# The output transfers of an eight-batch attention and gating kernel, issued from GpSimd's queue in the place of SyncE's

## The chip, the core and the metric

The kernel runs on one core of one Trainium2 chip. The metric is the device time of one execution in microseconds (us); lower is better. The core has TensorE (PE, with its weight loads as PEld), VectorE (DVE), ScalarE (ACT), GpSimd (POOL) and SyncE (SP). Each of them works through its own instructions in order. Transfers are issued by an instruction on one of the engines, and 16 DMA engines move the bytes.

## The reference

Eight batches, eight heads, 576 positions, 64 columns a head. Linear attention with a norm, then a gated feed-forward layer that mixes positions:

```python
kv = np.einsum('bhsd,bhse->bhde', k, v)
out = np.einsum('bhsd,bhde->bhse', q, kv)
rms = np.sqrt(np.mean(out * out, axis=-1, keepdims=True) + 1e-06)
out = out / rms * g_norm
x = out.transpose(0, 2, 1, 3).reshape(8, 576, 512)
h = np.maximum(x @ w_in, 0.0)                 # 512 -> 1024
u, v = h[..., :512], h[..., 512:]
v_n = (v - mean(v)) / np.sqrt(var(v) + 1e-06)
v_s = np.einsum('ts,bsd->btd', w_spatial, v_n) + b_spatial[None, :, None]
return (u * v_s) @ w_out                      # (8, 576, 512) float32
```

## The kernel before

**Tiling.** 576 positions are four blocks of 128 and a tail of 64. The tails of two batches, an even one and the odd one after it, share one block of 128. Every large product is made of three products of high and low parts (`hl`), which ACT makes by a rounding cast and DVE by a subtraction (`split`, lines 499 and 500); two of them, the one for `u` and the mix over positions, use a scheme of seven block products instead of eight (`seven`, `sp_steps`).

**Passes.** After an opening that decodes and splits the weights, `run` works through one batch at a time. In the text, pass b is that of batch b: `x_sums` makes sums of the attention output and splits them into the tiles `T` and `UX` (four ACT casts, line 499), `hv` makes `v` (psums `psh`, ACT line 469, DVE 475), `hv_tail` does the same for the tail block of two batches, `u_steps` makes `u` (psums `psua`, `psub`, `psuc`), `sp_steps` mixes and gates into `G`, and `out_unit` multiplies by `w_out`. The attention of batch b+1 (`pskv`, `KVB`, psums `pso` of line 190, `xx`, `xt`, `pstr`, `pstt`, ending in `XH` and `XL`) is mixed into pass b.

**The output.** `out_unit(b, c)` runs 12 matmuls into a PSUM bank (`pso` of line 463, one of four in the pool `ps_mm`), copies the bank to a tile `o` on ACT (line 805) and stores it. `o` is one of two buffers of the tag `stg`, which the attention tile `xt` of an odd batch shares. A pass ends with blocks 0, 1, 2, 3 where b is even, and with 0, 1, the shared tail block, 2, 3 where b is odd. So from the third block on a copy waits until an earlier `o` has been stored. The tail block is stored by two transfers of 64 rows (lines 809 and 810). Only the very last block is copied half by ACT and half by DVE (lines 802 and 803).

**What shares buffers.** `UX` and the output weight `WO` are one buffer, as are `T` and `G`: the load of `UX` (three transfers, line 1038, issued by POOL) waits for the last output matmul of the pass before, the casts into `T` as well; the load of `WO` (two transfers, line 1044, POOL) waits for the last use of `UX`. POOL also moves the tail tiles `TB` (line 549) and, in pass 1, stores three weight sums to `spare_u` (line 625).

**The order.** Within each engine the order is set by a scheduler that walks the program with a cost model of its own and picks what it takes to be ready; tokens in strings such as `EVEN` and `ODD` give the order in which the steps are written. A change of an instruction's engine can so move others.

Of the kernel before, what the change touches and what calls it, by code (L numbers as in the profile page):

```python
# [16 lines left out]
B, H, S, D = 8, 8, 576, 64  # L17
DM, FF = 512, 1024
FH = FF // 2
P = 128  # L20
NP = H // 2
NC = S // P
TAIL = S - NC * P
# [54 lines left out]
def body(ctx: ExitStack, tc, qT, kvm, kvt, g2, w_in, wsT, bsp, w_out, out):  # L78
    nc = tc.nc
# [379 lines left out]
    def three(ps, pairs):  # L459

        n = len(pairs)
        for i, (lt, rh) in enumerate(pairs):
            nc.tensor.matmul(ps, lt, rh, start=i == 0, stop=i == n - 1)  # L463

    def hl(lh, ll, rh, rl):
        return [(lh, rh), (lh, rl), (ll, rh)]
# [324 lines left out]
    def out_unit(b, c):  # L791
        ps = ps_mm.tile([P, 512], F32, name="pso2", tag="mm")
        cols = slice(c * P, (c + 1) * P)
        three(ps, [m for k in range(4) for m in
                   hl(*((GH[:, k, cols], GL[:, k, cols]) if c < NC else (GT[:, 0, k], GT[:, 1, k])),
                      WO[:, 0, k], WO[:, 1, k])])
        if (b, c % 2) == (B - 1, 0):
            o = work.tile([P, DM], F32, name="o", tag="v", bufs=3)
        else:
            o = work.tile([P, DM], F32, name="o", tag="stg", bufs=2)  # L800
        if (b, c) == (B - 1, NC - 1):
            nc.scalar.copy(o[:, 0:HALF], ps[:, 0:HALF])
            nc.vector.tensor_copy(o[:, HALF:DM], ps[:, HALF:DM])
        else:
            nc.scalar.copy(o, ps)  # L805
        if c < NC:
            nc.sync.dma_start(out[b, c * P:(c + 1) * P, :], o)
        else:
            nc.sync.dma_start(out[b - 1, NC * P:S, :], o[0:TAIL])
            nc.sync.dma_start(out[b, NC * P:S, :], o[TAIL:P])  # L810

# [298 lines left out]
    def outs(b):  # L1112
        return [lambda c=c: out_unit(b, c) for c in [0, 1] + [NC] * (b % 2) + [2, 3]]
# [54 lines left out]
```

## Time and profile before

| | |
|---|---|
| median of 3 runs | 487.5 us (487.13 to 489.95) |
| the profiled execution, its own time | 489.41 us |
| its span in the trace | 487.6 us |
| PE busy | 474.9 us, 97% |
| DVE busy | 381.4 us, 78% |
| ACT busy | 274.8 us, 56% |
| POOL busy | 35.8 us, 7% |
| TensorE's granted clock over the span | 0.997 |
| DMA queue of SP | 47.25 MB, 29.2% of 16 engines' span |
| DMA queue of POOL | 25.87 MB, 16.3% |

The profiled execution took 489.41 us, of which 1.8 us lie outside the span of its trace. It is 1.9 us above the median. Busy times are those of the trace; the ends of matmuls are modelled, so matmuls that follow each other overlap in the rows.

### The profile page before, as it was taken

How to read it: one execution, taken by the hardware profiler on the slowest of the kernel's cores; microseconds unless marked ns; L12 is line 12 of the kernel's file. 1: busy time of each engine (PE TensorE's matmuls, PEld its weight loads, DVE VectorE, ACT ScalarE, POOL GpSimd, SP SyncE). 2: the span in 40 equal slices, each digit the busy share in tenths (PEclk: the TensorE clock that was granted, in tenths of full speed). 3: DMA queues.
4: the chain of work that ended last, by engine and by line, in shares of the span. 5: the costliest groups of instructions: out<-in, count | busy, mean ns of one | idle time of the engine just before them, and what ended most of it. 6: DMA issues, size and time to landing. Idle time of an engine off the chain costs nothing.

```text
span 487.6 us, 10839 instructions
## 1 busy us (share of the span) xinstructions
PE 474.9 (97%) x4140; PEld 427.1 (88%) x4140; DVE 381.4 (78%) x1035; ACT 274.8 (56%) x824; POOL 35.8 (7%) x71
## 2 busy tenths in 40 slices
PE   6999989999999999999999999999999999999996
PEld 6889979998988899889988889888998889988995
DVE  2899787984994899869893899968986689986870
ACT  4898734975526773366533686257742578346322
POOL 5001100000211010000001001010000101010000
PEclk9999989999999999999999999999999999999999
DMA  8999331653159224390626616264323703333403
GB/s 284 375 301 318 90 99 67 184 182 109 65 174 315 87 77 173 123 333 12 217 85 196 206 46 206 84 218 164 116 103 130 239 1 80 128 88 128 149 26 108
DMA packets 30199, 74.16 MB, mean 152 GB/s; under 512 B 6626, under 2 KB 9698, under 8 KB 28612
## 3 DMA queue, kind: packets, MB, share of 16 engines
q1 hardware_dynamic: 24468, 47.25, 29.2%
q0 software_dynamic: 5456, 25.87, 16.3%
q8 instruction: 32, 0.52, 0.4%
q10 hardware_dynamic: 224, 0.36, 0.2%
q14 instruction: 19, 0.16, 0.1%
HBM read 58.09 MB, written 13.11 MB: 146 GB/s over the span
## 4 chain that ended last, share of the span: by engine, by line
PE 75%; DVE 11%; ACT 7%; DMA 4%; issue 2%; SPq 0%; ACTq 0%; DVEq 0%
PE pso L463 19%; PE psh L496 15%; PE psb L703 6%; PE psa L703 5%; PE psc L703 4%; PE psub L703 4%; PE psua L703 3%; PE psuc L703 3%; PE psu L463 3%; PE pstr L399 2%; PE pskv L190 2%; DMA stage<-w_out 2%; PE pso L190 2%; DVE TA L546 1%; DMA out<-o 1%
## 5 line engine op out<-in xcount | busy, mean ns | idle before, releaser
L463 PE MATMUL pso<-WO,G 128*128 128x512 f32 x384 | 94.3, 394 | 0.0
L463 PEld LDWEIGHTS pso<-WO,G 128*128 128x128 f32 x384 | 70.7, 188 | 14.5
L499 ACT CAST G<-SUMg 128x288 fp32r<-128x288 f32 (+1 forms) x56 | 22.6, 406 | 57.9 <-DVE SUMg L725 57.9
L805 ACT COPY o<-pso 128x512 f32<-128x512 f32 x35 | 19.6, 590 | 54.9 <-PE pso L463 40.4
L496 PE MATMUL psh<-WVH,XH 128*128 128x512 f32 x112 | 44.2, 395 | 0.0
L496 PE MATMUL psh<-WVL,XH 128*128 128x512 f32 x112 | 44.0, 393 | 0.0
L496 PE MATMUL psh<-WVH,XL 128*128 128x512 f32 x112 | 43.7, 390 | 0.0
L499 ACT CAST VH<-v 128x512 fp32r<-128x512 f32 (+1 forms) x60 | 33.4, 564 | 9.7 <-DVE v L528 5.0
L500 DVE TENSOR_TENSOR VL<-v,VH 128x512 fp32r<-128x512 f32 (+1 forms) x60 | 36.6, 614 | 2.3 <-ACT VH L499 1.5
L475 DVE BATCH_NORM_STATS2 s<-v 128x6 f32<-128x512 f32 x32 | 22.0, 688 | 11.8 <-ACT v L469 11.5
L483 ACT ACTIVATE v<-v,mv,rv 128x512 f32<-128x512 f32 x28 | 22.8, 814 | 7.6 <-DVE mv L482 7.5
L703 PE MATMUL psb<-WSH,VH 128*128 128x288 f32 x84 | 25.7, 306 | 0.0
L496 PEld LDWEIGHTS psh<-WVH,XL 128*128 128x128 f32 x112 | 21.0, 188 | 4.4
L703 PE MATMUL psb<-WSH,VL 128*128 128x288 f32 x84 | 24.8, 295 | 0.0
L496 PEld LDWEIGHTS psh<-WVH,XH 128*128 128x128 f32 x112 | 21.0, 188 | 4.3
L703 PE MATMUL psb<-WSL,VH 128*128 128x288 f32 x84 | 24.7, 295 | 0.0
L496 PEld LDWEIGHTS psh<-WVL,XH 128*128 128x128 f32 x112 | 21.0, 188 | 4.0
L500 DVE TENSOR_TENSOR G<-SUMg,G 128x288 fp32r<-128x288 f32 (+1 forms) x56 | 23.4, 419 | 1.1
L469 ACT ACTIVATE v<-psh 128x512 f32<-128x512 f32 x32 | 18.8, 590 | 6.5 <-PE psh L496 6.4
L392 ACT ACTIVATE XH<-pstr,gcol 128x512 fp32r<-128x512 f32 x28 | 18.3, 686 | 7.3 <-PE pstr L399 7.3
L500 DVE TENSOR_TENSOR T<-SUMu,T 128x576 fp32r<-128x576 f32 x12 | 9.0, 754 | 16.8 <-ACT T L499 11.5
L703 PE MATMUL psa<-WSH,VH 128*128 128x288 f32 x72 | 21.7, 302 | 0.4
(286 smaller groups left out, 1404.8 us busy)
## 6 DMA issues: line engine op xcount, KB each, us to landing
WO<-spare_o POOLq DMA_DIRECT2D x12, 1024.0 KB, 6.2
KV<-kvm SPq DMA_DIRECT2D x19, 512.0 KB, 5.9
UX<-spare_u POOLq DMA_DIRECT2D x18, 512.0 KB, 6.5
out<-o SPq DMA_DIRECT2D x32, 256.0 KB, 2.2
qt<-qT SPq DMA_DIRECT2D x28, 256.0 KB, 5.0
U<-kvm SPq DMA_DIRECT2D x12, 512.0 KB, 4.4
stage<-w_in SPq DMA_DIRECT2D x8, 512.0 KB, 7.3
stage<-w_out SPq DMA_DIRECT2D x4, 512.0 KB, 7.6
```

The source lines that it names most:

```text
L190: last[0] = nc.tensor.matmul(*args, **kw).ins
L392: nc.scalar.activation(hi, ps, AF.Copy, scale=gcol)
L399: nc.tensor.transpose(ps[:, c * P:(c + 1) * P], x[:, c * P:(c + 1) * P], ident)
L463: nc.tensor.matmul(ps, lt, rh, start=i == 0, stop=i == n - 1)
L469: nc.scalar.activation(v, ps, AF.Relu)
L475: nc.vector.bn_stats(s6, v)
L483: nc.scalar.activation(v, v, AF.Identity, bias=m, scale=r)
L496: nc.tensor.matmul(ps, lt, rh, start=k == 0 and i == 0, stop=k == NP - 1 and i == 2)
L499: nc.scalar.copy(hi, x)
L500: nc.vector.tensor_tensor(lo, x, f32(hi), op=ALU.subtract)
L703: nc.tensor.matmul(ps, lt, rh, start=start and i == 0, stop=stop and i == len(pairs) - 1, skip_group_check=True)
L805: nc.scalar.copy(o, ps)
```

## The change

The three places in `out_unit` that store a block of the output issue their transfers on POOL's queue and not on SP's. What is stored, from which tile and to where, stays.

```diff
         if c < NC:
-            nc.sync.dma_start(out[b, c * P:(c + 1) * P, :], o)
+            nc.gpsimd.dma_start(out[b, c * P:(c + 1) * P, :], o)
         else:
-            nc.sync.dma_start(out[b - 1, NC * P:S, :], o[0:TAIL])
-            nc.sync.dma_start(out[b, NC * P:S, :], o[TAIL:P])
+            nc.gpsimd.dma_start(out[b - 1, NC * P:S, :], o[0:TAIL])
+            nc.gpsimd.dma_start(out[b, NC * P:S, :], o[TAIL:P])
```

Forty transfers go from SP's queue, which keeps the loads of keys, values and queries, to POOL's. The scheduler sets some of the order anew, on PE, DVE and ACT too. Three places follow.

On POOL, the end of pass 1 to the end of pass 3 (`TB` are tail tiles, the two numbers name two of them):

```order
 L549 DMA TB_98<-TA_96 64x768
 L549 DMA TB_99<-TA_97 64x768
 L1044 DMA WO<-spare_o 128x2048 x2
+L807 DMA out<-o 128x512
+L1038 DMA UX<-spare_u 128x1024
+L807 DMA out<-o 128x512
+L1038 DMA UX<-spare_u 128x1024 x2
+L807 DMA out<-o 128x512 x2
+L1044 DMA WO<-spare_o 128x2048 x2
+L807 DMA out<-o 128x512 x2
+L809 DMA out<-o 64x512
+L810 DMA out<-o 64x512
```

The stores of pass 2 and 3 now stand between the loads of `UX` and `WO`; before, the loads stood there alone. In the other passes the three loads of `UX` stand behind all stores but the last one, and at the end of pass 6 behind the first two.

On ACT, the end of pass 3, where pass 4 begins. Before (`pso_3401` is the tail block, `pso_3434` block 3):

```order
L805 COPY o<-pso_3401 128x512
L805 COPY o<-pso_3418 128x512
L241 COPY KVB<-pskv 64x2x64 x2
L805 COPY o<-pso_3434 128x512
L499 CAST T<-SUMu_111 128x576
L499 CAST T<-SUMp_110 128x576
L499 CAST T<-SUMu_112 128x576
L499 CAST UX<-SUMg 128x576
L656 COPY U<-psua 128x288
L264 ACTIVATE xx<-pso 128x8x64 x2
```

The same place on ACT after the change:

```order
L805 COPY o<-pso_3401 128x512
L805 COPY o<-pso_3418 128x512
L241 COPY KVB<-pskv 64x2x64 x2
L499 CAST T<-SUMu_111 128x576
L499 CAST T<-SUMp_110 128x576
L499 CAST T<-SUMu_112 128x576
L499 CAST UX<-SUMg 128x576
L656 COPY U<-psua 128x288
L805 COPY o<-pso_3434 128x512
L264 ACTIVATE xx<-pso 128x8x64 x2
```

The copy of block 3 has moved behind the casts into `T` and the copy of `U`. At the start of pass 6 it stands behind two of the four casts; at the start of pass 2 it already stood behind them.

On PE, pass 4 after the change, at the first matmuls of `hv_tail` (`psh` of line 463):

```order
L399 MATMUL pstr<-ident,xx 128x128 x8
L703 MATMUL psua<-XH,WUH 128x288
L703 MATMUL psua<-XL,WUH 128x288
L703 MATMUL psua<-XH,WUL 128x288
L703 MATMUL psua<-XH,WUH 128x288
L703 MATMUL psua<-XL,WUH 128x288
L703 MATMUL psua<-XH,WUL 128x288
L463 MATMUL psh<-WVH,XH 128x512
L463 MATMUL psh<-WVL,XH 128x512
L703 MATMUL psuc<-T,UX 128x288 x6
```

Before, the six `psua` matmuls stood behind the six of `psuc`, and the first `hv_tail` matmul came right after the eight transposes `pstr`. Pass 6 has the same move.

## Rows read from the trace of the kernel before

**Rows 1.** The page's first part: busy time, share and instructions by engine.

```profile
PE 474.9 (97%) x4140; PEld 427.1 (88%) x4140; DVE 381.4 (78%) x1035; ACT 274.8 (56%) x824; POOL 35.8 (7%) x71
```

**Rows 2.** Busy time of PE, PEld, DVE, ACT, POOL by stretch, clock, DMA share, GB/s.

```profile
125.00:140.00 15.00, 14.75 (x95) 13.44 (x94) 14.84 (x45) 7.37 (x22) 3.99 (x6) 1.00 0.27 90
151.00:206.00 55.00, 54.86 (x467) 49.06 (x467) 48.40 (x132) 32.08 (x100) 3.84 (x7) 1.00 0.42 139
264.70:321.00 56.30, 55.30 (x465) 49.17 (x465) 48.29 (x132) 32.02 (x100) 3.77 (x7) 1.00 0.42 137
379.90:434.60 54.70, 54.58 (x456) 49.07 (x455) 48.40 (x132) 31.68 (x99) 3.79 (x7) 1.00 0.27 90
434.60:487.60 53.00, 49.05 (x292) 44.27 (x291) 31.25 (x85) 21.74 (x49) 2.67 (x5) 1.00 0.35 115
```

**Rows 3.** Waits: who waited for whom, us in total, times, longest.

```profile
ACT o L805 <- DMA out<-o: 12.6, 7, 3.6
...
PE pskv L277 <- DMA KV<-kvm: 1.9, 3, 0.8
...
PE psh L463 <- ACT XH L392: 0.7, 1, 0.7
```

**Rows 4.** Waits of SP's queue, same columns.

```profile
SPq L807 <- ACT o L805: 142.5, 16, 50.5
```

**Rows 5.** ACT in time, pass 3 to 4: start, us, instruction, [idle before <- releaser].

```profile
258.39 1.07 ACT L805 COPY o<-pso 128x512 f32<-128x512 f32 x2 [5.81 <-PE pso L463]
...
261.12 1.28 ACT L805 COPY o<-pso 128x512 f32<-128x512 f32 x2 [1.65 <-DMA out<-o]
...
266.50 0.58 ACT L805 COPY o<-pso 128x512 f32<-128x512 f32 x1 [3.65 <-DMA out<-o]
266.98 0.68 ACT L499 CAST T<-SUMu 128x576 fp32r<-128x576 f32 x1
...
278.21 0.46 ACT L392 ACTIVATE XH<-pstt,gcol 128x256 fp32r<-128x256 f32 x1
```

**Rows 6.** ACT in time, the starts of passes 2 and 6.

```profile
151.09 0.67 ACT L499 CAST T<-SUMu 128x576 fp32r<-128x576 f32 x1 [1.07 <-PE pso L463]
...
380.03 0.59 ACT L805 COPY o<-pso 128x512 f32<-128x512 f32 x1 [2.15 <-DMA out<-o]
380.52 0.68 ACT L499 CAST T<-SUMu 128x576 fp32r<-128x576 f32 x1
...
391.74 0.46 ACT L392 ACTIVATE XH<-pstt,gcol 128x256 fp32r<-128x256 f32 x1
```

**Rows 7.** The chain that ended last, in order of time: start, us, what.

```profile
262.25 4.15 DMA out<-o
```

**Rows 8.** PE in time: first `hv_tail` matmul of pass 6, first uses of `UX`.

```profile
279.30 0.96 PE L703 MATMUL psuc<-T,UX 128*128 128x288 f32 x6
...
392.85 0.48 PE L463 MATMUL psh<-WVH,XH 128*128 128x512 f32 x1
...
444.99 0.96 PE L703 MATMUL psuc<-T,UX 128*128 128x288 f32 x6
```

**Rows 9.** DMA issues: KB each, median us from issue to landing.

```profile
UX<-spare_u POOLq DMA_DIRECT2D x18, 512.0 KB, 6.5
out<-o SPq DMA_DIRECT2D x32, 256.0 KB, 2.2
...
spare_u<-VH POOLq DMA_DIRECT2D x2, 256.0 KB, 3.0
...
WTH<-WTH POOLq DMA_DIRECT2D x1, 144.0 KB, 8.2
```

**Rows 10.** POOL in time: its issues of transfers.

```profile
126.63 0.54 POOL L625 DMA_DIRECT2D spare_u<-VL  x1 [0.54 <-DVE VL L500]
...
265.28 1.59 POOL L1038 DMA_DIRECT2D UX<-spare_u  x3 [29.68 <-PE pso L463]
...
434.99 1.60 POOL L1038 DMA_DIRECT2D UX<-spare_u  x3 [22.64 <-PE pso L463]
```

**Rows 11.** SP, ACT and DVE in time, the last block of the output.

```profile
482.58 2.30 SPq L807 DMA_DIRECT2D out<-o  x2
483.69 0.37 ACT L802 COPY o<-pso 128x256 f32<-128x256 f32 x1 [1.85 <-PE pso L463]
484.09 0.42 DVE L803 COPY o<-pso 128x256 f32<-128x256 f32 x1 [9.87 <-ACT o L802]
```

## The prediction

> **What bounds the kernel now.** I read the busy times first, then the busy times by stretch, then the waits, then ACT and the transfers in time at the ends of passes. PE is busy for 474.9 of 487.6 us [rows 1]; its clock is at the full level in every stretch from 125 us on [rows 2]. So the kernel is bound by PE, and the question is not how long SP or ACT wait but which of their waits reach PE. Of the passes I compare the even ones in the middle, which do the same work: pass 2 (151.0 to 206.0, 55.0 us), pass 4 (264.7 to 321.0, 56.3 us) and pass 6 (379.9 to 434.6, 54.7 us) [rows 2]. PE is idle for 0.14, 1.00 and 0.12 us in them. From 434.6 on it is idle for 3.95 us, nearly all of it after its last matmul: ACT starts on the last block at 483.69 [rows 11] and the span ends at 487.6.
>
> The waits look larger than what they cost. SP stands for 142.5 us in front of output stores that wait for ACT's copies [rows 4], and loads stand behind them. But the only loads that PE is seen to wait for are keys in line 277, 1.9 us in three waits of at most 0.8 [rows 3], and that line belongs to the opening, ahead of the first store. So SP's blocked queue costs PE nothing that I can see. ACT waits for 12.6 us, seven times, until a store has landed and its `o` buffer is free [rows 3]; this reaches PE at one place. At the end of pass 3 the two transfers of the tail block are issued beside the loads of keys, the second takes 4.15 us to land [rows 7], and the copy of block 3 waits 3.65 us for it, until 266.50 [rows 5]. Behind it on ACT stand the casts into `T`, at 266.98, 2.3 us after PE is done with the pass. From the first cast to the `XH` of the tail block the rows show a chain of fixed length, 266.98 to 278.21, 11.2 us [rows 5], and in pass 6 380.52 to 391.74, also 11.2 us [rows 6]. In pass 6 `XH` ends at 392.20 and PE takes it at 392.85 [rows 6, 8], so PE has some 0.6 us in hand there; in pass 4 it has none and waits 0.7 us [rows 3].
>
> **The change part by part.** *Forty issues leave SP.* Nothing on the path waits for SP's loads, so I count 0; the bounds are 0 and the 1.26 us of idle PE time in the three even passes [rows 2].
>
> *The new order on ACT at the start of pass 4.* The copy of block 3 now stands behind the four casts and a copy, so the casts start when PE is done with `G`, near 264.7 (as in pass 2, where the first cast starts at 151.09, released by PE [rows 6]). The casts take some 2.3 us, the copy of `U` 0.3, so block 3 is copied near 267.3, with `XH` about 11.8 us after the casts begin, at 276.5 in the place of 278.2. In passes 4 and 6 PE also reaches `hv_tail` six matmuls later, some 0.8 us by the row of six that spans 0.96 us with its last end [rows 8]. The wait in pass 4 goes. What it gives is the idle time that pass 4 has over passes 2 and 6, 1.00 less 0.13, so 0.9 us; the lower bound is 0, the upper one the whole excess of the pass, 56.3 less 54.7, 1.6 us [rows 2]. I take 0.9, since an idle PE is what the mechanism removes.
>
> *Stores land later from POOL.* A store of the same 256 KB issued by POOL took 3.0 us to land, against 2.2 for SP's [rows 9]. In the passes this delays ACT, which waits for `o`. Counted with 3.0 us for both transfers in turn: at the end of pass 3 block 0 is issued at 259.0 and lands at 262.0, the tail block is copied by 262.6, its two stores are issued 0.55 us apart (POOL takes 1.60 us for three issues [rows 10]) and land by 266.2, and block 3 is wanted at 267.3: covered by 1.1 us. At the end of pass 5 the same count gives 381.2 against 381.1, covered by `XH`'s slack of 0.6 plus the 0.8 of the six moved matmuls. At the end of pass 1 it gives 153.0 against 153.8. So 0 us, with little cover in the last two. At the end of even passes the casts wait longer after passes 4 and 6, but `T` and `UX` are first needed much later (in pass 7 at 444.99, ten us after PE begins it [rows 8]). Less than nothing can come out as well: POOL's queue is another one than the loads of keys use, so the 4.15 us of the tail block may shrink.
>
> *POOL's loads behind the stores.* `UX` now waits for the stores ahead of it, which wait for ACT. Before, it was issued at 265.28 and 434.99 [rows 10]; with 6.5 us to land [rows 9] that is 271.8 and 441.5, against first uses at 279.30 and 444.99 [rows 8], so 7.5 and 3.5 us of cover. Pass 7 has the least, and there only two stores stand ahead, copied as soon as PE has finished them. At the end of passes 2 and 4 the third store waits for the first to land, some 3 us, of which the cover takes all. I count 0; without the cover it would be up to 3 us, twice.
>
> *The end.* The last store lands on the path. It costs 3.0 less 2.2, so 0.8 us; the bounds are 0, since POOL has nothing queued ahead, and 6.0, from the 8.2 us that a POOL transfer took in the busy opening [rows 9]. I take 0.8, because by then no load runs beside it. The Trainium skill (DMA: Bandwidth & Descriptors, Specifications) gives a first byte after about 1 us on GpSimd's path and about 0.6 on SyncE's; by it this term would be an estimated 0.4 us. The two rows agree with its sign.
>
> *The rest of the order.* PE, DVE and ACT have some instructions in another order in passes 2 to 7. No row prices that. Like passes differ by at most 1.6 us [rows 2], which bounds it on both sides; I take 0.
>
> The sum is 0.8 less 0.9, so -0.1 us against the profiled execution's span of 487.6 us and its own 489.41. That execution is 1.9 us above the median of the runs, and I put the same change on the median: **487.4 us**. A measurement of this kernel can tell about 1%, 4.9 us, from no change.
>
> **The rivals.** *A: the stores land so late that ACT holds up PE (slower).* The landing L counts twice at the end of an odd pass, since the tail block's copy waits for block 0 and block 3's copy for the tail block. With `XH`'s slack, 0.6 us at pass 2 and 1.4 at passes 4 and 6, PE begins to wait at L above (154.4 - 147.0) / 2 = 3.7, (268.7 - 260.2) / 2 = 4.3 and (382.5 - 375.2) / 2 = 3.65 us. Halfway between the two POOL rows, at 5.6 us [rows 9], the three passes lose 3.8, 2.6 and 3.9 us, 10.3 in all, and the time would be 497.7 us; at 4.5 us they lose 3.7, and it would be 491.1. For it speaks the 4.15 us that SP's own store took beside loads [rows 7]; against it, that the first landing of each pair meets an idle queue. Chance 0.12 for a time over 1%.
>
> *B: DVE slows POOL's issues.* In the stretch from 125 to 140 us DVE is busy for 14.84 of 15 us, and POOL's issue at 126.63 still takes 0.54 us [rows 2, 10], as much as one of three in 1.60. So an issue costs the same beside a full DVE. The Trainium skill says otherwise (DMA: Bandwidth & Descriptors, SWDGE vs HWDGE vs iDMA): GpSimd writes its descriptors into rings in SBUF, and DVE locks it out of SBUF in two-port modes, while transfers issued by SP are immune. By that rule the 40 issues would stretch while `x_sums` runs on DVE; the trace does not bear it out. Were each issue doubled to 1.1 us, the two tail stores would come 1.1 us later in each odd pass: by the count above nothing is lost in pass 4, some 0.5 us in passes 2 and 6 together, and 0.5 at the end: 488.4 us. Chance 0.04, inside the 1%.
>
> *C: SP's free queue or the new order gives PE time (faster).* From 151 us on PE is idle for some 5.2 us, of which 3.9 lie behind its last matmul. All the rest recovered and the end unchanged gives 486.2 us. For a gain of 1% the path would need 4.9 us that no row shows idle. Chance 0.03 for that.
>
> **How the numbers follow.** The forecast, with rival B and the small end of rivals A and C, keeps within 1%: 0.85. Slower by over 1%: 0.12, rival A with a landing above some 4.8 us. Faster by over 1%: 0.03. The range goes from 485.5 us, the 1.6 us of the pass's excess and 0.4 us by which the fastest run lies below the median, to 491.2 us, rival A at 4.5 us.
>
> **What would show it.** Right: in the changed kernel the first cast of pass 4 starts within 0.3 us of PE's last output matmul and PE no longer waits for `XH` there; pass 4 is within 0.5 us of passes 2 and 6; stores issued by POOL land after some 3 us; the last copy to the end of the span is some 0.8 us longer; SP's wait for ACT's `o` is gone and no pass is shorter for it. Wrong: a PE wait for `XH` at the start of passes 2 or 6 with ACT held by a store, landings above 4 us at the ends of odd passes, or a wait of `psuc` for `UX`.

## The result, and the profile after

The changed kernel takes **492.08 us** (median of 16 runs, 490.4 to 498.52) against 487.61 us (16 runs, 486.4 to 491.34) for the kernel before, measured on the same chip: a ratio of 1.0091, with a 95% interval of 1.0068 to 1.0114. That is 4.5 us slower, 0.9 us beyond the top of the range. The profiled execution has a span of 494.9 us and took 496.77. It is one of the longer runs: eleven of the 16 lie between 490.4 and 492.3, five between 495.2 and 498.5.

The page's first part of the changed kernel answers to [rows 1]. POOL has 22.0 us more for 40 more instructions, 0.55 us an issue, as in [rows 10]:

```profile
PE 479.8 (97%) x4140; PEld 429.6 (87%) x4140; DVE 381.6 (77%) x1035; ACT 274.0 (55%) x824; POOL 57.8 (12%) x111
```

For the comparison I cut both traces into passes: from the first output matmul (`pso` of line 463) of one pass to that of the next, and from that of pass 7 to the end of the span. The pieces of the changed kernel, passes 2 to 7 and the end, with the columns of [rows 2]:

```profile
133.96:198.18 64.22, 62.12 (x550) 55.00 (x549) 50.44 (x138) 34.39 (x107) 10.05 (x17) 0.97 0.48 157
198.18:252.25 54.07, 53.63 (x518) 48.38 (x517) 44.00 (x122) 28.78 (x93) 4.89 (x9) 1.00 0.45 154
252.25:313.74 61.49, 61.04 (x555) 54.12 (x554) 49.98 (x137) 34.44 (x105) 7.10 (x13) 1.00 0.44 146
313.74:367.63 53.89, 53.88 (x518) 48.43 (x517) 43.15 (x121) 28.81 (x92) 4.87 (x9) 1.00 0.45 155
367.63:428.92 61.29, 60.81 (x554) 54.03 (x553) 50.04 (x137) 34.32 (x105) 7.10 (x13) 1.00 0.34 115
428.92:475.23 46.31, 46.31 (x283) 42.38 (x281) 36.29 (x92) 20.30 (x46) 4.90 (x9) 1.00 0.30 103
475.23:494.90 19.67, 14.98 (x70) 12.14 (x68) 5.49 (x16) 4.37 (x12) 3.29 (x6) 1.00 0.20 67
```

The same cuts of the kernel before, and of a second profile of the changed one (run e1 below), in us:

| | pass 2 | 3 | 4 | 5 | 6 | 7 | end |
|---|---|---|---|---|---|---|---|
| before | 60.29 | 53.13 | 61.90 | 53.14 | 60.70 | 46.31 | 18.93 |
| changed | 64.22 | 54.07 | 61.49 | 53.89 | 61.29 | 46.31 | 19.67 |
| changed, e1 | 61.01 | 57.56 | 61.69 | 53.90 | 61.30 | 46.31 | 19.63 |

The 7.3 us between the two spans are 3.9 in pass 2, 0.9 in pass 3, -0.4 in pass 4, 0.75 and 0.6 in passes 5 and 6, 0.7 at the end, and 0.8 in the opening. All of those 0.8 us lie ahead of the first output matmul (106.71 against 105.95 us), where the code is the same; over all profiles of this study the opening ends anywhere between 131.1 and 135.0 us. Passes 4 to 7 and the end agree between the two profiles of the changed kernel to 0.2 us. Passes 2 and 3 do not: some 5 us are lost there, most of it in pass 2 in the first profile and in pass 3 in the second.

**Pass 2.** ACT in time, in the changed kernel, at the start of passes 2 and 4 (answers to [rows 5, 6]):

```profile
149.75 0.59 ACT L805 COPY o<-pso 128x512 f32<-128x512 f32 x1 [2.65 <-DMA out<-o]
...
152.29 0.59 ACT L805 COPY o<-pso 128x512 f32<-128x512 f32 x1 [1.51 <-DMA out<-o]
...
157.56 0.59 ACT L805 COPY o<-pso 128x512 f32<-128x512 f32 x1 [2.09 <-DMA out<-o]
...
270.72 0.67 ACT L499 CAST T<-SUMu 128x576 fp32r<-128x576 f32 x1 [1.09 <-PE pso L463]
...
273.85 0.59 ACT L805 COPY o<-pso 128x512 f32<-128x512 f32 x1 [0.31 <-DMA out<-o]
```

The chain of waits across the start of pass 2 (answers to [rows 7]):

```profile
146.92 2.75 DMA out<-o
...
151.18 6.28 DMA out<-o
...
166.78 0.37 ACT XH L392
...
167.20 1.22 PE psh L463 x2
```

Block 0's store takes 2.75 us to land and lets the tail block be copied at 149.75. The tail's second store takes 6.28 us, and block 3's copy waits for it until 157.56. The attention tiles behind it on ACT end in `XH`, which PE waits for.

The copy at 152.29 is that of block 2, and the store that it waits for is block 1's: 4.65 us from POOL, against 2.54 from SP in the kernel before, where the same copy came 2.5 us sooner after the start of the piece:

```profile
148.99 0.59 ACT L805 COPY o<-pso 128x512 f32<-128x512 f32 x1 [0.39 <-DMA out<-o]
```

The casts into `T` stand behind it on ACT. The changed kernel's waits in total:

```profile
PE psh L463 <- ACT XH L392: 1.6, 1, 1.6
...
ACT o L805 <- DMA out<-o: 17.5, 11, 2.6
```

They are to be held against [rows 3]. Then PE's clock, in stretches of 2 us (busy time and count of PE, granted clock, DMA share, GB/s):

```profile
162.00:164.00 2.00, 2.00 (x16) 1.00 0.89 293
164.00:166.00 2.00, 1.24 (x10) 1.00 0.13 41
166.00:168.00 2.00, 0.80 (x2) 0.77 0.00 0
168.00:170.00 2.00, 2.00 (x9) 0.50 0.00 0
170.00:172.00 2.00, 2.00 (x12) 0.88 0.00 0
```

After 1.96 us of idle PE in 4 us the clock stands at its lower level, 1.2 GHz, for a few us; 0.23, 0.50 and 0.12 of 2 us each are 1.7 us lost. Idle time and clock together are 3.7 of the 3.9 us, against 0.14 us of idle time in the same piece before.

**What the loads do there.** SP in time, at the end of pass 1, in the kernel before:

```profile
147.26 0.83 SPq L156 DMA_DIRECT2D KV<-kvm  x2
148.62 0.51 SPq L809 DMA_DIRECT2D out<-o  x1
149.19 0.59 SPq L810 DMA_DIRECT2D out<-o  x1
149.87 0.54 SPq L807 DMA_DIRECT2D out<-o  x1
150.50 1.45 SPq L162 DMA_DIRECT2D KT<-kvt  x2
```

The same place in the changed kernel, SP and then POOL:

```profile
148.03 0.82 SPq L156 DMA_DIRECT2D KV<-kvm  x2
148.95 1.38 SPq L162 DMA_DIRECT2D KT<-kvt  x2
```

```profile
150.63 0.54 POOL L809 DMA_DIRECT2D out<-o  x1 [2.52 <-ACT KVB L241]
151.18 0.55 POOL L810 DMA_DIRECT2D out<-o  x1
153.29 0.56 POOL L807 DMA_DIRECT2D out<-o  x1 [1.57 <-DMA KT<-kvt]
```

Before, SP's order held the two `KT` loads back until the stores of the tail block and of block 2 had been issued. Now no store stands ahead of them, and they are sent at 148.95 and 149.47, 1.7 and 1.2 us ahead of the tail's first store. In the second profile of the changed kernel only one of them is ahead of it, and the tail's two stores land after 4.4 and 4.5 us. The store of block 1, too, now leaves closer to the loads: 0.5 us ahead of the first `KV` (147.56 and 148.03) against 0.9 before (146.35 and 147.26).

**The landings** over the whole run (answers to [rows 9]) have a median that says little:

```profile
out<-o POOLq DMA_DIRECT2D x32, 256.0 KB, 2.7
out<-o POOLq DMA_DIRECT2D x8, 128.0 KB, 3.5
```

A store that meets no load lands after 2.2 to 2.7 us (the ends of passes 5 and 7), beside loads of keys after 4.4 to 6.6 (the ends of passes 1 and 3), and between or behind loads of `UX` in its own queue after 6 to 10. SP's stores beside those loads were no quicker: in the kernel before, block 3's store took 6.5, 8.3, 8.7 and 9.0 us at the ends of passes 1 to 4.

**The end.** From the end of the last copy to the end of the span it is 3.8 us (DVE's copy at 490.65, 0.42 long, span 494.9) against 3.1 by [rows 11]. The last issue, in the changed kernel and in the kernel before:

```profile
491.48 0.55 POOL L807 DMA_DIRECT2D out<-o  x1 [1.44 <-DVE o L803]
```

```profile
484.55 0.34 SPq L807 DMA_DIRECT2D out<-o  x1
```

### The profile page after: what moved, and what is told of

The parts are those of the page before. It is cut to its first block, busy times and chain, and to the rows that moved or that the text cites. A ratio compares the mean times of both kernels' runs of the same rounds, so it can differ in the third digit from the quotient of the medians.

```text
span 494.9 us, 10819 instructions
## 1 busy us (share of the span) xinstructions
PE 479.8 (97%) x4140; PEld 429.6 (87%) x4140; DVE 381.6 (77%) x1035; ACT 274.0 (55%) x824; POOL 57.8 (12%) x111
## 4 chain that ended last, share of the span: by engine, by line
PE 53%; issue 17%; DVE 13%; ACT 9%; DMA 5%; POOL 2%; POOLq 0%; SPq 0%; DVEq 0%; ACTq 0%
PE pso L463 15%; PE psh L496 11%; PE psb L703 5%; PE psc L703 4%; PE psa L703 3%; PE psub L703 3%; PE psuc L703 2%; PE psua L703 2%; DMA stage<-w_out 2%; DVE VL L500 2%; DMA out<-o 2%; PE pskv L190 2%; DVE XL L393 1%; PE pso L190 1%; DVE s L475 1%
## 5 line engine op out<-in xcount | busy, mean ns | idle before, releaser
L807 POOL DMA_DIRECT2D out<-o x32 | 17.7, 554 | 211.1 <-ACT o L805 197.0
L393 DVE SCALAR_TENSOR_TENSOR XL<-pstr,gcol,XH 128x512 fp32r<-128x512 f32 x28 | 20.6, 744 | 1.5 <-ACT XH L392 1.3
```

Source lines behind the costliest of these rows:

```text
L393: nc.vector.scalar_tensor_tensor(lo, ps, gcol, f32(hi), op0=ALU.mult, op1=ALU.subtract)
L807: nc.gpsimd.dma_start(out[b, c * P:(c + 1) * P, :], o)
```

## The experiments

All ratios are to the kernel before, measured beside each run. "The tail" stands for the two stores of the shared tail block. Times of passes and landings are those of one profile of each run.

**e1, the changed kernel again**, for the spread.

> The changed kernel once more, for a second trace. Theory M (the stores of pass 1's tail block land late beside the loads of keys, ACT's copy of block 3 waits, PE waits for XH at hv_tail of pass 2 and then runs at a lower granted clock): the tail stores of pass 1 land after more than 5 us, PE waits 1 to 2 us at hv_tail of pass 2, and pass 2 is 2 to 4 us longer than before. Theory N (the new order on PE, DVE and ACT costs the time): pass 2, whose PE order is nearly the old one, is within 1 us of before, and passes 3 to 7 carry the loss.

One run, 494.92 us, span 492.9; its passes are in the table above. The tail landed after 4.4 and 4.5 us, ACT waited little for it, and PE showed hardly any wait for `XH`, so neither theory's picture of pass 2 came; pass 2 is 0.7 us longer even so. ACT in time:

```profile
153.03 0.59 ACT L805 COPY o<-pso 128x512 f32<-128x512 f32 x1 [0.36 <-DMA out<-o]
```

Pass 3 is the one that loses here. ACT in time:

```profile
208.99 0.59 ACT L805 COPY o<-pso 128x512 f32<-128x512 f32 x1 [1.78 <-DMA out<-o]
...
215.58 0.59 ACT L805 COPY o<-pso 128x512 f32<-128x512 f32 x1 [4.84 <-DMA out<-o]
```

Block 1's store of pass 2, issued at 205.81 between two loads of `UX`, lands after 9.7 us; block 3's copy waits 4.84 us for it, and behind that copy stand those of `v` and `U`; PE waits for one of `U`. PE in time:

```profile
222.88 0.46 PE L703 MATMUL psua<-XH,WUH 128*128 128x288 f32 x1 [2.07 <-ACT U L656]
```

Its clock over the next 2 us stretches from 222 is 0.77, 0.50 and 0.88, the same 1.7 us as in pass 2 of the first profile.

**e2, only pass 1's stores by POOL; e3, all but pass 1's; e4, the changed kernel with the tail block's `o` in another tag.**

```diff
 e2  (nc.gpsimd if b == 1 else nc.sync).dma_start(out[...], ...)
 e3  (nc.sync if b == 1 else nc.gpsimd).dma_start(out[...], ...)
 e4  if (b, c % 2) == (B - 1, 0) or (c == NC and b < B - 1):   # o in tag v
```

> Only the stores of pass 1 go by POOL, all others by SP; PE and DVE keep the order of the kernel before. Theory M: 490 to 491.5 us, nearly the whole loss, with tail stores that land after 5 us or more and a PE wait at hv_tail of pass 2. Theory N: 487.6 us, as before.

489.14 us, 1.0014 (0.9991 to 1.0037). Pass 2 61.41, all others within 0.35 us of before. Theory M's 490 us did not come: the tail took 4.6 to 4.7 us, and PE waited 0.4 us for `XH`.

> All stores by POOL but those of pass 1, which go by SP; PE and DVE keep the order of the changed kernel. Theory M: 488 to 489.5 us, what is left is the last store and small losses in odd passes. Theory N: 491 to 492 us, as the changed kernel.

491.24 us, 1.0046 (1.002 to 1.0073). Pass 2 61.00, pass 3 54.51, pass 4 61.30, pass 5 53.89, pass 6 61.30, end 19.73. This is theory N's number and not M's: without pass 1's stores about half of the loss is left, in pass 3 and in the parts that do not vary. Pass 2 lost 0.7 us as well, though its stores and their order on SP are those of the kernel before, with both `KT` loads behind them: the tail took 5.6 and 5.3 us, and block 3's copy waited for it (ACT in time):

```profile
153.52 0.59 ACT L805 COPY o<-pso 128x512 f32<-128x512 f32 x1 [0.70 <-DMA out<-o]
```

> The changed kernel with the shared tail block copied to a buffer of the tag v (three buffers) in place of one of the two of stg, so that block 3's copy waits for block 1's store and no longer for the tail's. The scheduler orders PE and DVE anew as well. Theory M: ACT's waits for stores shrink from 17.5 us to under 10, no PE wait at hv_tail of pass 2, 487.5 to 489 us. Theory N: it depends on the order it gets, no gain in pass 2 in particular.

503.59 us, 1.03 (1.0258 to 1.0342). This one is no test of its question: the scheduler gave PE another order in each of the passes 2 to 6, and PE waits in new places.

**e6, one store alone; e7, all by POOL but passes 1 and 2; e9, less key data; e5, the third queue.**

```diff
 e6  (nc.gpsimd if (b, c) == (2, 1) else nc.sync).dma_start(out[...], o)
 e7  (nc.sync if b in (1, 2) else nc.gpsimd).dma_start(out[...], ...)
 e9  for i, j in ... ((0, 1 if b >= 3 and not in_u(b, p) else NC),):   # a quarter of these KV loads
 e5  nc.scalar.dma_start(out[...], ...)
```

> The kernel before with one transfer moved: block 1's store of pass 2 goes by POOL, between the first and the second load of UX. PE and DVE keep their order. Theory Q (what the change costs at random comes from stores that share POOL's queue with UX and run beside the loads of keys): the store lands after 6 to 10 us in the place of some 3, ACT's copy of block 3 waits 2 to 5 us, PE waits 0 to 2.5 us for ACT early in pass 3 and may fall to the lower clock after it: 488 to 491.5 us. Theory N (the new order alone): as before, 487.5 to 489.

489.18 us, 1.0008 (0.9979 to 1.0037). That store landed after 4.8 us, and pass 3 lasted 53.13: no loss.

> All stores by POOL but those of passes 1 and 2, so that passes 2 and 3 start as before, while passes 4 to 7 have the order of the changed kernel. Theory Q: passes 2 and 3 are within 0.7 us of before, what is left is 0.75 us at the end and some 0.7 us each in passes 5 and 6, 1.5 to 2 us over before, and no PE wait above 1 us after 125 us. Theory N alone: 3.5 us or more over before, as the changed kernel.

490.67 us, 1.0022 (0.9989 to 1.0054). Passes 2 and 3 are those of before (60.30, 53.13); pass 4 61.30, pass 5 53.89, pass 6 61.30, end 19.66. This is the part of the change that does not vary: -0.6, +0.75, +0.6 and +0.7, 1.5 us. It shows in the passes; the ratio alone can't be told from no change.

> The changed kernel with a quarter of the key and value loads of batches 3 to 7 in the pairs 0 and 1 (128 KB in the place of 512 KB each; the rest of those keys is stale). PE and DVE keep the order of the changed kernel. Theory Q with the loads of keys as the rival for the DMA engines: the tail stores at the end of pass 1 and block 1's store of pass 2 land within 5 us, no PE wait above 1 us in passes 2 and 3, 1.5 to 2.5 us over before. If UX alone holds the stores up: block 1's store of pass 2 still takes 6 us or more. If POOL's path itself is slow: landings as in the changed kernel, 4 to 6.6 us.

493.32 us, 1.008 (1.005 to 1.0109). It leaves out three quarters of these loads, so its output is another one. The tail's stores of pass 1 landed after 2.6 us and pass 2 lasted 60.28: with little key data beside them they are on time. Block 1's store of pass 2 still took 6.2, and pass 3 lasted 55.27. The two losses are apart.

> All stores issued on ACT's queue, which is neither SP's with the loads of keys nor POOL's with UX. The scheduler orders PE, DVE and ACT anew. Theory Q: stores land in 2 to 5 us, none at 6 or more behind UX; ACT spends 0.35 to 0.6 us on each of 40 issues, 16 us in all, and the time is 487 to 491 us. If only POOL's way of issuing is slow: landings at 2.2 us throughout and 487 to 488 us. Theory N: depends on the order it gets.

489.12 us, 1.0015 (0.9985 to 1.0044). From ACT's queue nothing measurable is lost; pass 3 is 53.13, the end 18.96. PE's order differs in passes 2, 4 and 6, so the passes are no clean comparison: pass 2 is 1.0 us longer (the tail's second store took 5.2 us), pass 4 1.1 us shorter.

**e10, pass 2's stores alone; e11 and e12, the late stores back to SP; e8, the kernel before with the tail's `o` in the other tag.**

```diff
 e10  (nc.gpsimd if b == 2 else nc.sync).dma_start(out[...], ...)
 e11  the tail's two:  (nc.sync if b == 1 else nc.gpsimd).dma_start(out[...], ...)
 e12  as e11, and     (nc.sync if (b, c) == (2, 1) else nc.gpsimd).dma_start(out[...], o)
 e8   if (b, c % 2) == (B - 1, 0) or (c == NC and b < B - 1):   # stores by nc.sync
```

> The kernel before, with the four stores of pass 2 by POOL and all others by SP. PE and DVE get the changed kernel's order in pass 3, and the order of before everywhere else. Theory: pass 2 and passes 4 to 7 as before (60.3, 61.9, 53.1, 60.7, 46.3, end 18.9); pass 3 alone is longer, 54.0 to 57.5 us against 53.1: 0.5 to 0.9 us of it by the new order, which does not vary, and the rest by how late block 1's store lands between the loads of UX (6 us or more). Median 488.5 to 490 us, ratio 1.002 to 1.005. Rival (the order is harmless in pass 3, only the late store costs): with a landing under 5 us pass 3 is 53.1 us. Rival (the store is harmless, as in the run in which only that store was moved): pass 3 is 53.5 to 54.1 us however late it lands.

492.04 us, 1.0062 (1.0031 to 1.0093). In the profile (span 488.0 us) pass 3 is 54.33, the others within 0.4 us of before; block 1's store landed after 6.2 us. The ten runs go from 489.15 to 495.02.

> The changed kernel, with nothing but the two transfers of pass 1's tail block back on SP's queue; the instructions of PE, DVE and ACT keep the changed kernel's order. On SP the two stand behind the loads KV (two) and one KT, with one KT behind them, so the bytes that are sent ahead of them and beside them are nearly the changed kernel's. Theory Q (a store loses when its own queue is not the one that the loads use: both queues are then served side by side, and the 256 KB wait for most of the 1.3 MB; in the same queue they go in their turn): they land within 3.5 us of their issue, ACT's copy of block 3 no longer waits for them, and pass 2 lasts 60.3 us, against 64.2 and 61.0 in the two profiles of the changed kernel; pass 3 keeps its 54 to 57.5 us, passes 5 and 6 and the end keep their 53.9, 61.3 and 19.7. Median some 490.5 us, 1.006 of before. Rival M (the loads themselves, whichever queue the store is in, since they are now sent ahead of it): the landing stays at 5 us or more, pass 2 at 61 to 64 us, and the median at 492.

493.03 us, 1.009 (1.0056 to 1.0124). **Theory Q fell.** The tail's stores, now on SP behind two `KV` and one `KT`, took 5.0 and 4.7 us, where Q wanted 3.5 at most. Pass 2 lasted 61.40, with a PE wait of 0.4 us for `XH`.

> The kernel of the run before, with block 1's store of pass 2 on SP's queue as well. This brings the order of PE and DVE in pass 3 back to that of the kernel before; the order of the other passes stays the changed kernel's. Theory (the change's loss is two stores that land late, with a fixed part of the new order behind them): pass 2 lasts 60.3 us, pass 3 53.1, pass 4 61.3, pass 5 53.9, pass 6 61.3, the end 19.7: +1.5 us on the kernel before, some 489.2 us, ratio 1.003. If pass 3 keeps over 54 us with that order and that queue, the store of block 1 is not its cause. If the ratio stays at 1.008, the loss sits in places that I have not named.

494.64 us, 1.0119 (1.0073 to 1.0164). Pass 3 came back (53.15), but pass 2 lasted 64.65. The tail took 5.8 us, and yet block 3's copy did not wait for it. What came late is block 1's store, from POOL, with 5.9 us: the first row is block 2's copy, which waited for it. Block 2's own store, issued 0.9 us later, took 5.9 us again, and the attention tile `xt`, which shares the buffers of `o`, waited for that one. ACT in time:

```profile
154.17 0.59 ACT L805 COPY o<-pso 128x512 f32<-128x512 f32 x1 [2.79 <-DMA out<-o]
...
161.07 0.59 ACT L377 ACTIVATE xt<-pst 128x128 f32<-128x128 f32 x2 [2.25 <-DMA out<-o]
```

So the tail lands late from SP's queue as well (e3, e11, e12), and it is not the only store that can cost pass 2 its 4 us.

> The kernel before (all stores by SP), with the tail block's o in a buffer of the tag v, as in the last pass of even blocks, so that block 3's copy no longer waits for the tail's store. PE, DVE and POOL keep the order of before; on ACT and SP the tail's copy and its stores come first in passes 1, 3 and 5. Theory: the only place of the kernel before at which a store reaches PE is the start of pass 4, where PE waits 0.7 us for XH; that wait goes and pass 4 is 0.7 to 1.0 us shorter (61.0 us), all else the same: 486.6 us, ratio 0.998, too little to tell from no change in the median but not in the length of the pass. Rival: v's buffers are now short, and DVE waits for one at the start of passes 2, 4 and 6: 488 us or more.

487.87 us, 0.9975 (0.9954 to 0.9996): 0.25% faster than the kernel before, about what the theory says and at the edge of what can be measured. Block 3's copy at the end of pass 3 is released by PE and no longer by a store (ACT in time), and pass 4, from 245.12 to 305.82, lasts 60.70 us with 0.13 us of idle PE, 1.2 us less than before. Pass 2 is 0.6 us longer (60.85):

```profile
263.45 0.59 ACT L805 COPY o<-pso 128x512 f32<-128x512 f32 x1 [1.56 <-PE pso L463]
```

```profile
245.12:305.82 60.70, 60.57 (x554) 54.07 (x553) 49.62 (x136) 34.26 (x105) 3.79 (x7) 1.00 0.45 148
```

**e13, keys and stores in one queue again, POOL's; e14, also at the end of pass 2; e15, less `KT`; e16, the kernel before with `KT` sent early.**

```diff
 e13  KV and KT: (nc.gpsimd if b == 4 and p < 2 else nc.sync).dma_start(...)
 e14  KV and KT: (nc.gpsimd if 4 <= b < 6 and p < 2 else nc.sync).dma_start(...)
 e15  w = 32 if b > 3 else P
      nc.sync.dma_start(kt[0:w], kvt[b, p:p + 2].rearrange(...)[0:w])
 e16  KT: (nc.gpsimd if b == 4 else nc.sync).dma_start(kt, ...)   # stores by nc.sync
```

> The changed kernel, with three loads of keys at the end of pass 1 (two KV, one KT) in POOL's queue too, where they stand behind the stores of blocks 0 and 1 and ahead of the tail block's. This is the order that SP's queue had in the kernel before, in another queue; one KT stays on SP. The order of PE, DVE and ACT is that of the changed kernel. Theory S (stores and loads in one queue are sent in turn; in two queues the stores share the 16 engines with 1 MB of keys): the stores of blocks 0 and 1 land within 2.7 us, the tail block is copied a us sooner, its stores land within 4 us, and pass 2 lasts 60.3 us, against 61.0 to 64.2. Pass 3 keeps 54 us or more. Median 490 to 491 us, ratio 1.004 to 1.006. Rival L (it is enough that the keys are sent ahead of the tail, whichever queue they use): the tail lands after 4.7 us or more, as from SP behind the keys, and pass 2 stays at 61 us or more; median 492.

495.15 us, 1.013 (1.0074 to 1.0187). **Theory S fell** as well: the tail's stores took 7.2 us, pass 2 64.81, the clock fell (0.53 over the 2 us from 166).

> The run before, with the three loads of keys at the end of pass 2 in POOL's queue as well, behind block 1's store and the loads of UX. This brings back the order of PE and DVE that pass 3 had in the kernel before, while all its stores are POOL's and block 1's still stands behind one load of UX. If the new order is what costs in pass 3: 53.1 us, though block 1's store lands after 6 us or more. If the late store costs by itself: 53.6 us or more. Passes 5 and 6 and the end keep 53.9, 61.3 and 19.7 us in both. By the first, with pass 2 at 60.3, the median is some 489.5 us.

497.63 us, 1.0193 (1.0152 to 1.0233). Pass 3 lasted 54.54 with the order that PE and DVE had in the kernel before, so late stores cost by themselves. Block 1's store landed after 6.2 us, block 3 was copied after a wait of 2.50 us, DVE's `XL` came late behind ACT, and PE waited for it (PE in time; the row reads word for word the same, at 235.14, in the changed kernel):

```profile
235.06 1.16 PE L190 MATMUL pso<-KVB,qt 64*64 64x64 f32 x62 [0.40 <-DVE XL L393]
```

> The changed kernel, with every KT load of batches 4 to 7 cut to a quarter (32 of 128 KB, the other rows keep older keys), so this computes something else. All five engines keep the changed kernel's order. Theory T (the two KT loads, which SP now sends ahead of the tail block's store and used to hold back until block 2 was stored, make the tail late): the tail's stores of pass 1 land within 4 us against 6.5, block 3's copy no longer waits for them, pass 2 lasts 60.3 us. Pass 3 keeps 54 us or more, since block 1's store stands behind a load of UX and not behind KT. Median some 490.5 us, ratio 1.005. Rival V (the megabyte of KV does it, as the run with a quarter of it suggests): the tail lands after 5 us or more, pass 2 stays at 61 us or more, median 492.

492.06 us, 1.0094 (1.0056 to 1.0131). It leaves out three quarters of each `KT`. The tail took 4.5 and 4.3 us. That is less than the 6.6 and 6.3 of the changed kernel's first profile, but its second (e1) has 4.4 and 4.5 with the full `KT`, so the landing says nothing for theory T. ACT copies block 3 at 153.38 with no wait for a store; passes 2 and 3 of the profile are

```profile
131.97:192.89 60.92, 60.56 (x551) 53.69 (x549) 50.34 (x138) 34.48 (x107) 10.05 (x17) 1.00 0.49 162
192.89:247.16 54.27, 53.84 (x518) 48.44 (x517) 44.00 (x122) 28.77 (x93) 4.91 (x9) 1.00 0.44 150
```

Theory T expected pass 2 at 60.3 and a ratio of 1.005; neither came. What still delays pass 2 is block 1's store, 4.7 us from POOL: block 2's copy waits for it, and the casts and block 3's copy stand behind that one (ACT in time; this kernel has one line more):

```profile
150.31 0.59 ACT L806 COPY o<-pso 128x512 f32<-128x512 f32 x1 [1.75 <-DMA out<-o]
```

> The kernel before, all stores by SP, with the two KT loads of the end of pass 1 on POOL's queue, which is idle there, so that they are sent before the tail block's store and not after block 2's. PE, DVE and ACT keep the order of before. Theory T: the tail's stores land after 4.5 us or more against some 2.5, though no store has changed its queue, and pass 2 lasts 60.7 to 64 us against 60.3; everything else stays as before; ratio 1.001 to 1.006. Rival (the stores' own queue is what makes them late): they land within 3 us and pass 2 lasts 60.3 us.

490.4 us, 1.0025 (1.0002 to 1.0049). No store has changed its queue, and the tail's second one takes 5.1 us (the chain of waits), so that ACT now waits for it at block 3:

```profile
147.60 5.11 DMA out<-o
```

```profile
152.78 0.59 ACT L805 COPY o<-pso 128x512 f32<-128x512 f32 x1 [0.44 <-DMA out<-o]
```

In the kernel before this copy has no wait: its tail's stores had landed by 153.80, within 4.6 us. But 5.1 us is less than the 5.3 and 5.6 of e3, where no `KT` was ahead, so this run does not show that the early loads do it either. Pass 2 is 60.79, 0.5 us longer.

**The profiles with one order of PE and of `o` in pass 2, side by side** (without e4, e5 and e8). Copies are told in us after the start of the piece, landings in us from the issue; a landing that the trace does not tell is bounded by block 3's copy.

| | `KT` loads ahead of the tail's first store | the tail's second store | block 2 copied | block 3 copied | pass 2 |
|---|---|---|---|---|---|
| e9, a quarter of `KV` | 2 | 2.6 | 17.7 | 20.48 | 60.28 |
| before, e6, e7 | 0 | at most 4.6 | 15.8 to 16.1 | 20.60 | 60.29 to 60.30 |
| e10 | 0 | at most 4.6 | 15.9 | 20.75 | 60.46 |
| e16 | 1 | 5.1 | 15.8 | 21.27 | 60.79 |
| e15, a quarter of `KT` | 1 | 4.3 | 18.3 | 21.41 | 60.92 |
| e1 | 1 | 4.5 | 18.0 | 21.53 | 61.01 |
| e3 | 0 | 5.3 | 16.0 | 21.56 | 61.00 |
| e11 | 1 | 4.7 | 18.6 | 21.88 | 61.40 |
| e2 | 1 | 4.7 | 18.5 | 21.94 | 61.41 |
| e12 | 1 | 5.5 | 19.6 | 22.68 | 64.65 |
| changed | 2 | 6.3 | 18.3 | 23.60 | 64.22 |
| e14 | 2 | 6.4 | 17.7 | 23.80 | 64.50 |
| e13 | 2 | 7.0 | 17.7 | 24.24 | 64.81 |

Pass 2 lasts the longer the later ACT copies block 3; only e12, with its `xt`, stands out of the row. Two stores delay that copy. One is the tail. The other is block 1's: wherever pass 1's stores of blocks 0 to 2 are POOL's it took 4.0 to 5.9 us, and block 2 was copied at 17.7 or later, where SP's took 2.5 to 2.8 as far as the traces tell it, and block 2 was copied at 16.1 or sooner.

## Why the prediction was wrong, point by point

**Failed: "Stores land later from POOL", counted at 0.** The step took 3.0 us for both transfers in turn, from a POOL store of the opening, and found 0.8 us of cover at the end of pass 1. Alone, a POOL store lands even sooner, in 2.2 to 2.7 us. But at the end of pass 1 the tail's second store took 6.3 us in the first profile (4.4 to 7.0 in the others with the full loads), ACT copied block 3 three us later than before, and PE stood idle for 2.0 us. The step also followed blocks 0, tail and 3 alone: block 1's store, which holds up block 2's copy and the casts behind it, went from 2.5 to 4.0 us and more, and was in no term. So its price was a lone store's, where the stores met the loads of keys. The signs that the prediction had named for being wrong came: the wait for `XH` in pass 2 with ACT held by a store, and landings above 4 us at the ends of passes 1 and 3.

That the loads of keys beside it make the tail late is shown by e9: with a quarter of `KV` it landed after 2.6 us, with all else as in the changed kernel. What was not counted either is what SP does with its freedom: I had booked its blocked queue as a cost that PE does not see, and it was also an order that kept the `KT` loads behind the stores. What these two loads add is not shown. The three profiles of full loads with both of them ahead of the tail have it land after 6.3 to 7.0 us; with one ahead it is 4.5 to 5.5, and with none 4.4 (e7) to 5.3 (e3), so one makes no difference that can be seen. e15 and e16, made to test this, do not stand apart from runs without their edit. That it is the tail's own queue was the rival, and e3, e11 and e12 speak against it, since from SP's queue the tail took 4.7 to 5.8 us; for block 1's store, which was late from POOL in every run, the queue and its closer distance to the loads were not told apart.

**Rival A was the mechanism.** It let PE wait once two landings at the end of pass 1 exceed 7.4 us together. They were 9.0, 9.1 and 9.6 us in the first profile, e14 and e13, so 1.6, 1.7 and 2.2 over, and PE's idle time around `XH` was 2.0, 2.2 and 2.5 us. So the count is right to some 0.4 us; it also missed small losses below its threshold (e1 with 7.0, e2 with 7.2), which come with block 1's store. It priced only the wait. The clock took 1.7 us more.

**Failed: the end of even passes.** The text held that a late store there delays only casts that are needed much later. At the end of pass 2 block 1's store stands between loads of `UX`, takes 6 to 10 us, and holds up block 3's copy, behind which stand `v` and `U` copies that DVE and PE want soon. Pass 3 lost 0.9 to 4.4 us where that store landed after 6 us or more (the changed kernel, e1, e3, e9, e10, e11, e13, e14, e15), and nothing where it landed after 4.8 or sooner (e6, e7, e12). Of these only e14 has the late store in the old order of PE, and it lost 1.4 us. The new order with an early store was not run, so what the order itself adds in pass 3 is open.

**Failed in size: the rest of the order, taken as 0.** Passes 5 and 6 are longer by 0.75 and 0.6 us in each profile in which their stores are POOL's (e4, with yet another order, apart). In pass 5 PE is busy for 53.88 of 53.89 us, so the rows show no wait. That the new order does it is argued and not tested: every such profile has the new order and POOL's stores together. Nor does a full row exclude short waits, since the ends of matmuls are modelled: pass 2 of e15, in the order of before, is 0.63 us longer and shows only 0.22 us of that as idle time. The two together lie within the 1.6 us that the step gave as its bound.

**Right in the mechanism, half in size: pass 4.** The first cast starts at 270.72, released by PE's last output matmul and not by a store; block 3's copy stands behind the casts with a wait of 0.31 us, and the only wait for `XH` left is that in pass 2. The pass gains 0.4 us in the profile, up to 0.6 in others, against 0.9 forecast; 0.55 us less idle time is what is visible. With the old order the pass itself lasts anything from 61.4 (e16) to 62.2 us (e2).

**Right by luck in part: the end,** 0.74 us against 0.8, by another split. The landing is 2.3 us and not 3.0, against 2.0 for SP's last store, so it gives 0.3; POOL's issue starts 0.41 us after the copy's end where SP's starts 0.04 after it, which gives 0.4 that no term held.

**Right: the loads of `UX` behind the stores,** 0: no `psuc` waits for `UX` in any profile. **Right: SP's wait** is gone, and no pass is shorter for it. **Rival B** did not come: the Trainium skill (DMA: Bandwidth & Descriptors, SWDGE vs HWDGE vs iDMA) has GpSimd locked out of its descriptor writes while DVE runs in a two-port mode. With DVE busy for 77% of the span the 40 issues took 0.54 to 0.57 us each, as before; no row tells in which mode DVE ran.

**The sum.** The part that does not vary is +1.5 us (e7). The rest of the 4.5 us, some 3 on the median, is passes 2 and 3, which lost 4.9 and 5.1 us in the two profiles; the runs, from 490.4 to 498.5 us, say that it is less in most. **Still open:** why the same program lands the same store after 6 us in one run and after 10 in another, and the tail after 4.4 or 6.3; what share the early `KT` loads and POOL's queue itself have in that; and what costs passes 5 and 6 their 0.7 us.

## What to carry to other kernels

A queue that is blocked by waiting stores also keeps the loads behind them from being sent; before freeing it, ask what it will send sooner. Price each store at its landing time beside the traffic that it meets, not at that of a lone one. Where a chain of buffers passes through several landings, follow every one of them, and sum them against the slack; that count was right to some 0.4 us here. If a store gates a buffer, another buffer can be worth more than another queue: e8 gained 0.25%, though the same edit on the changed kernel (e4) came with another order and cost 3%.

## What the runs showed of the hardware

A PE wait of 1.6 to 2.1 us was followed by a stretch at the lower clock in the changed kernel and in e1 (granted 0.77, 0.50 and 0.88 in three stretches of 2 us, 1.7 us lost), which nearly doubles what the wait costs; in e13 and e14 it fell after a wait of 1.6 us too. It need not: in e12 PE waited 1.6 us for `XH` and was idle for 3.1 us within 8 (0.42, 0.38, 0.90 and 1.39 us in four stretches of 2 us), and the clock stayed at 1.00.

The same 256 KB took from 2 to 10 us to land, whichever engine issued it: 2.3 to 10.5 from POOL (e1), 2.0 to 9.0 from SP (before), 2.0 to 10.2 from ACT (e5). Stores from ACT's queue were no quicker than SP's (the first one of a pass 2.0 to 2.1 us, those beside loads mostly 4 to 10), and nothing measurable was lost there.
